# Which engine takes out a weight's sign and in how many bits, what fills the first routing phase, and how the first expert's first products are cut

## The chip, the cores and the metric

The kernel runs on one core of a Trainium2 chip. The metric is the device time of one execution in microseconds (us), median over runs; lower is better. Engines are named as the profile names them: PE (TensorE matmul, PEld its weight load), DVE (VectorE), ACT (ScalarE), POOL (GpSimd), SP (SyncE, which here only starts DMAs).

## The reference, cut to what matters

```python
x = attention(q, k, v)                  # 4 x 8 heads x 576 rows, window of 64; -> 2304 tokens x 512
logits = x @ w_gate                     # 8 experts, at most 288 tokens each
# all (token, expert) pairs in order of falling logit; a token goes to the first expert with room
out[mask_e] = relu(x[mask_e] @ w1[e]) @ w2[e]          # expert: 512 -> 1024 -> 512
h = out @ w_in                          # 512 -> 2048
y = maximum(0.01 * h, h) @ w_out        # 2048 -> 512, the output
```

`w_in` and `w_out` come to the kernel as 64-bit floats. The kernel has to make 32-bit floats of them on the chip.

## The kernel before, in words

**Attention** comes first, in 18 chunks of 128 tokens (to about 96 us). Then one list of steps is walked (`Moe.run`, L982): expert 0 (8 steps), expert 1 (8), block 0 of the last layer (16 steps, 512 tokens), experts 2 and 3, block 1, and so on. A step is `hstep` (first product and its non-linearity, `h` then `hh`) and `ystep` (second product, into `ya` for an expert, `oa` for a block). PE gets `h` of step i+1 before the second product of step i. Expert 0 multiplies in plain f32; all later steps split both factors into a high and a low part (ACT casts the high part, DVE or POOL subtracts it) and add three products.

**Routing** is worked out in 8 phases, one expert per phase (`Router.phase`, L357). A phase is a chain: six times DVE compares (`r_ge`), PE counts in 18 small matmuls (`rp`), DVE compares with the room left (`r_sat`), PE, DVE (`r_ns`); then prefix sums, and at the end the token numbers (`ids`). Expert 0 cannot begin before phase 0 has ended: its rows are gathered (`xg`, POOL DMAs), transposed on PE (`xtp`), copied by ACT (`xT`), and only then multiplied. Phase 1 runs during expert 0, phases 2 and 3 during expert 1 and block 0.

**Conversion** (`Convert`, L587) turns the 64-bit weights into 32-bit ones in 32 units of 128x512, two per step of a block. A unit arrives in a `cv_in` tile (4 of them) as pairs of 32-bit words, low and high. `open` (L617) has three ACT operations: k=0 scales the high word, read as f32, by 2^-112 into the result; k=1 takes the top byte of the low word and writes the three missing bits; k=2 writes the scaled result as f16, whose only surviving bit is the sign. Both k=1 and k=2 write 16 bits each into halves of the same 32-bit word. `join` (L644) is one DVE operation: result shifted left by 3, or that word. Units 0, 1, 4, 5, 8, 9 and 12 to 17 (`KEPT`) are converted in place, then cast by ACT (`cast`) and their low part taken by DVE (`low`) into `res`. The other twenty get one of six `cv_r` tiles, are split in block 0 (`split`, L761) and sent to DRAM (`wsp`); a tile is free again when the unit six before it was split. Units 0 to 2 are done during attention (`spare`, L691), unit 3's ACT operations at its end.

**The order of the work** is planned when the kernel is built. `Clocks` (L1089) keeps a modelled time per engine from a cost per operation; `Convert.acts` opens units and issues casts while ACT's modelled time is no more than 200 ns ahead; `Convert.piece` issues one `join` or `low` on DVE if its inputs are due. `RouteDriver.tick` (L1200), called between groups of matmuls, chooses between split low parts, routing and conversion pieces. `RouteDriver.finish` (L1224) runs routing phases that must be complete, and in phases 0 and 1 calls `nfill` pieces at marked points. Each engine takes its instructions strictly in the order issued, so an instruction that waits holds back all behind it on that engine. No conversion loads are issued from the end of phase 0 (`hold`) until step 2 of expert 0. Nearly all instructions after attention are recorded under one line, L1158, so the rows are read by tile names.

Of the kernel before, what the change touches and what calls it, by code (L numbers as in the profile page):

```python
# [6 lines left out]
F32 = mybir.dt.float32  # L7
F32R = mybir.dt.float32r
BF = mybir.dt.bfloat16
I32 = mybir.dt.int32  # L10
AF = mybir.ActivationFunctionType
ALU = mybir.AluOpType
# [542 lines left out]
    return out  # L555


U8, U16, F16 = mybir.dt.uint8, mybir.dt.uint16, mybir.dt.float16

def lay_w12(w1, w2):  # L560
    a = w1.reshape(NE, 4, 128, 8, 128).transpose(0, 3, 2, 1, 4).reshape(NE, 8, 128, 512)
# [18 lines left out]
NRING = 6  # L580
# [6 lines left out]
class Convert:  # L587
# [5 lines left out]
    def __init__(self, nc, pool, wio, res):  # L593
        self.nc, self.pool, self.wio, self.res = nc, pool, wio, res
        self.st, self.nl, self.done, self.hold = {}, 0, 0, False
        self.side = nc.scalar.copy, nc.vector
        self.out, self.taken, self.due, self.came, self.now = {}, set(), [], {}, lambda: 0
        self.left, self.joined, self.relief = {}, [], lambda: None
    def load(self, eng=None):
        n = self.nl  # L600
        if n >= 32 or self.hold:
# [15 lines left out]
    def open(self, n):  # L617

        if n not in self.out:
            while n not in self.st:  # L620
                self.load()
            self.out[n], self.left[n] = self.room(n), [2, 1, 0]
        t, o, act = self.st[n], self.out[n], self.nc.scalar.activation
        half = t.rearrange("p a b -> p (a b)").bitcast(F16).rearrange("p (a b) -> p a b", b=4)
        k = self.left[n].pop()
        if k == 0:
            act(o, t[:, :, 1].bitcast(F32), AF.Copy, scale=float(2.0 ** -112))
        elif k == 1:
            act(half[:, :, 0].bitcast(U16), t.bitcast(U8)[:, :, 3], AF.Copy, scale=1 / 32, bias=-31 / 64)
        else:  # L630
            act(half[:, :, 1], o, AF.Copy)
    def done_at(self, ap):
# [10 lines left out]
        self.load()  # L643
    def join(self):  # L644
        n = self.done
        o = self.out[n].bitcast(I32)
        self.nc.vector.scalar_tensor_tensor(out=o, in0=o, scalar=3, in1=self.st.pop(n)[:, :, 0], op0=ALU.logical_shift_left, op1=ALU.bitwise_or)
        self.done += 1
        if n in KEPT:
            self.joined.append(n)  # L650
        else:
            self.load()
# [23 lines left out]
    def until(self, n):  # L676
        while self.done < min(n, 32):
            u = self.done
            if u not in self.out and not self.free(u):
                self.relief()  # L680
                self.finish(u)
            while u not in self.out or self.left[u]:
                self.open(u)
            self.join()
        self.finish(n)
    def finish(self, n):
        while self.joined and self.joined[0] < n:
# [3 lines left out]
    def spare(self, n):  # L691

        g, v, act = self.nc.gpsimd, self.nc.vector, self.nc.scalar.activation
        while self.done < n:
            k = self.done
            t, o = self.st[k], self.room(k)
            self.out[k], self.left[k] = o, []
            lo, hi, oi = t[:, :, 0], t[:, :, 1], o.bitcast(I32)
            half = t.rearrange("p a b -> p (a b)").bitcast(F16).rearrange("p (a b) -> p a b", b=4)
            act(o, hi.bitcast(F32), AF.Copy, scale=float(2.0 ** -112))  # L700
            yield
            act(half[:, :, 0].bitcast(U16), t.bitcast(U8)[:, :, 3], AF.Copy, scale=1 / 32, bias=-31 / 64)
            yield
            act(half[:, :, 1], o, AF.Copy)
            yield
            v.scalar_tensor_tensor(out=oi, in0=oi, scalar=3, in1=lo, op0=ALU.logical_shift_left, op1=ALU.bitwise_or)
            del self.st[k]
            yield
            if k in KEPT:
                w = self.res[KEPT.index(k)]  # L710
                g.tensor_copy(w[:, 0], o)
                yield
                g.tensor_tensor(out=w[:, 1], in0=o, in1=w[:, 0].bitcast(F32), op=ALU.subtract)
            self.load()
            yield
            self.done += 1
# [2 lines left out]
XM = 4, 3, 2  # L719
PAIR = 2  # L720
ELOW, MLOW = 1, 1
WARM, CVG = 11, 2
XW = 5200
class Moe:
    def __init__(self, nc, tc, ctx, ident, pp_misc, pa, pp, w12, wsp, xd, idl, out, route):
# [80 lines left out]
    def xtrans(self, n, a):  # L806
        nc = self.nc
        if a == 0:
            self.xT[n] = [self.wk.tile([128, 3, 4, 96], F32R, tag=f"xT{d}", name=f"xT{n}_{d}", bufs=1) for d in range(2)]
        hi, lo = self.xT[n]  # L810
        self.route.flush(("x", n))
        g = self.xg.pop((n, a))
        if n < 2 and n + a == 2 or a == 1 and (n % 2 or n == 0):
            pt = self.pp.tile([128, 4, 96], F32, tag="h", name=f"xtp{n}_{a}")
        else:
            pt = self.misc.tile([128, 4, 96], F32, tag="xt", name=f"xtp{n}_{a}", bufs=1)
        for k in range(4):
            nc.tensor.transpose(pt[:, k, :], g[:, 128 * k:128 * k + 128], self.ident[0:96, 0:96])
        if n == 0:
            nc.scalar.copy(hi[:, a].bitcast(F32), pt)  # L820
            return
        nc.scalar.copy(hi[:, a], pt)
        self.route.later(("x", n), hi, lambda: nc.vector.tensor_tensor(out=lo[:, a], in0=pt, in1=hi[:, a].bitcast(F32), op=ALU.subtract))
    def mslots(self, n):
        return 512 * n, 512 if n < 4 else 256
    def hprod(self, i, hi):

        nc = self.nc
        kind, n, p, f = self.seq[i]
        lo = self.hdone.get(i, 0)  # L830
        self.hdone[i] = hi
        if i not in self.ph:
            self.ph[i] = self.pp.tile([128, 512], F32, tag="h", name=f"h{i}")
        ph, w = self.ph[i], self.w[i, 0]
        self.route.flush(("w", i, 0))
        if kind == "e":
            self.route.flush(("x", n))
        if kind == "e" and n == 0:
            for k in range(4):
                nc.tensor.matmul(ph[:, :288].rearrange("p (a c) -> p a c", a=3), w[:, 128 * k:128 * k + 128], self.xT[n][0][:, :, k].bitcast(F32), start=(k == 0), stop=(k == 3))  # L840
                self.route.tick()
            return
        whi, wlo = w[:, 0], w[:, 1]
        if kind == "e":
            N = 288
            rh, rl = ([x[:, :, k, :] for k in range(4)] for x in self.xT[n])
        else:
            s0, N = self.mslots(n)
            pos = s0 % RING
            rh, rl = ([y[k][pos // 512][:, pos % 512:pos % 512 + N] for k in range(4)] for y in self.Y)  # L850
        o = ph[:, :N].rearrange("p (a c) -> p a c", a=3) if kind == "e" else ph[:, :N]
        prods = [x for k in range(4) for x in ((whi, rh, k), (whi, rl, k), (wlo, rh, k))]
        if (lo, hi) != (0, 12) or p == 0:

            prods.sort(key=lambda x: x[1] is rl)
        for j, (w, r, k) in enumerate(prods):
            if lo <= j < hi:
                nc.tensor.matmul(o, w[:, 128 * k:128 * k + 128], r[k], start=(j == 0), stop=(j == 11))
                if j % 3 == 2:
                    self.route.tick()  # L860
# [121 lines left out]
    def run(self):  # L982
        nc, seq, R = self.nc, self.seq, self.route
# [23 lines left out]
            self.conv.piece()  # L1007
        for a in range(3):
            self.xtrans(0, a)
        self.hstep(0)  # L1010
        self.split(2, 0)
        self.split(1, 1)
        for i in range(n):
# [9 lines left out]
            for m in range(1, 8):  # L1023
# [9 lines left out]
                        self.xtrans(m, a)  # L1033
                if i == first[m] - 1 and seq[i][0] == "e":
                    self.xtrans(m, 2)
            if i == 2:

                self.conv.hold = False
                while len(self.conv.st) < 3:
                    self.conv.load()  # L1040

            for j in range(i + 1, i + 6 if self.ng > 1 else min(i + 6, first[1] + 2)):
# [42 lines left out]


CVA, CV0, CVL = 3, 8, 3
AHEAD, SOON, ASLACK = 2, 150, 200
class Clocks:  # L1089


# [18 lines left out]
    def cost(self, e, name, out, ins):  # L1110
# [5 lines left out]
            return max(n[0] * (1.68 if ins[0].dtype == F32 and ins[1].dtype == F32 and ins[1].shape != ins[0].shape else 0.447) + 1, 25)  # L1116
        n = max(n)
        if e == "scalar":
            return n * 0.833 + (55 if psum else 93)
        if e == "gpsimd":  # L1120
            return n * 2.2 + 98
        big = [x for x in ins if x.shape[-1] > 1]
# [38 lines left out]
class RouteDriver:  # L1161
# [38 lines left out]
    def tick(self):  # L1200
        for _ in range(4):
            t, dve = self.nc.at["tensor"], self.nc.at["vector"]
            one = self.ph == 1
            go = [j for j in self.jobs if j[1] <= max(t, dve)]
            go = [j for j in go if not isinstance(j[0], tuple)] or go
            soon = [j for j in self.jobs if not isinstance(j[0], tuple) and j[1] <= max(t, dve) + self.HOLD]
# [17 lines left out]
    def finish(self, ph, known=None):  # L1224

        k = 0
        while 'ids' not in self.out.get(ph, ()):
            self.piece()
            if known and ph in self.out:
                known()  # L1230
                known = None
            k += 1
            if ph <= 1:
                for _ in range(self.nfill):
                    self.conv.piece()

def build(nc, tc, qT, kT, v, vT, wg, cfd, cid, cbd, w12, wio, out):
    with ExitStack() as ctx:
# [65 lines left out]
        pm = ctx.enter_context(tc.tile_pool(name="pm", bufs=1, space=PSUM, reuse_waits="tile"))  # L1304
        ph = ctx.enter_context(tc.tile_pool(name="m_ph", bufs=2, space=PSUM, reuse_waits="tile"))
        nc = cv.nc = rt.nc = Clocks(nc)
        cv.side = nc.scalar.copy, nc.vector
        cv.now = lambda: max(nc.at["tensor"], nc.at["vector"])
        R = RouteDriver(nc, rt, cv)
# [29 lines left out]
```

## Time and profile before

| | us |
|---|---|
| median of 3 runs | 840.31 (838.67 to 843.12) |
| the profiled execution, time | 840.8 |
| its span, first to last instruction | 839.1 |
| PE busy | 770.2 (92%) |
| DVE busy | 437.6 (52%) |
| ACT busy | 380.5 (45%) |

In the stage tables a row gives the stretch in us from the span's start, its length, the busy time of each engine with the number of instructions, the granted TensorE clock as a share of 2.4 GHz, the DMA share and GB/s. In a timeline a row gives the start, the duration, the engine, the operation with its output and input tiles and count, and in brackets how long the engine sat idle before it and what ended that.

### The profile page before, as it was taken

How to read it: one execution, taken by the hardware profiler on the slowest of the kernel's cores; microseconds unless marked ns; L12 is line 12 of the kernel's file. 1: busy time of each engine (PE TensorE's matmuls, PEld its weight loads, DVE VectorE, ACT ScalarE, POOL GpSimd, SP SyncE). 2: the span in 40 equal slices, each digit the busy share in tenths (PEclk: the TensorE clock that was granted, in tenths of full speed). 3: DMA queues.
4: the chain of work that ended last, by engine and by line, in shares of the span. 5: the costliest groups of instructions: out<-in, count | busy, mean ns of one | idle time of the engine just before them, and what ended most of it. 6: DMA issues, size and time to landing. Idle time of an engine off the chain costs nothing.

```text
span 839.1 us, 15086 instructions
## 1 busy us (share of the span) xinstructions
PE 770.2 (92%) x5828; PEld 639.0 (76%) x5829; DVE 437.6 (52%) x1191; ACT 380.5 (45%) x771; POOL 138.9 (17%) x165
## 2 busy tenths in 40 slices
PE   6987629979988989999999999999999999999996
PEld 4765425668866668899777789998888998888896
DVE  3656685668865677697766833322223323222332
ACT  5788991177686663342211134532124453221222
POOL 2323002010010000300000027720004761000200
PEclk9999855999999999999999999999999999999999
DMA  9994243565464445848322428682243935223652
GB/s 346 411 405 151 75 143 125 176 200 131 126 231 157 142 176 176 163 151 172 121 81 76 151 93 177 191 226 74 104 178 110 216 93 209 101 101 121 234 197 102
DMA packets 44728, 138.70 MB, mean 165 GB/s; under 512 B 9712, under 2 KB 10608, under 8 KB 44656
## 3 DMA queue, kind: packets, MB, share of 16 engines
q1 hardware_dynamic: 40816, 126.36, 45.6%
q0 software_dynamic: 3408, 11.01, 5.1%
q8 instruction: 46, 0.75, 0.4%
q10 hardware_dynamic: 432, 0.36, 0.1%
q14 instruction: 26, 0.21, 0.1%
HBM read 117.78 MB, written 19.93 MB: 164 GB/s over the span
## 4 chain that ended last, share of the span: by engine, by line
PE 48%; DVE 6%; issue 5%; DMA 5%; ACT 4%; POOL 1%; POOLq 0%; SPq 0%; ACTq 0%
PE h L1158 23%; PE oa L1158 16%; PE ya L1158 6%; DMA raw<-in_w_dram 3%; ACT cv_in L1158 3%; PE rp L1158 2%; DVE w L1158 1%; DVE r_ob L1158 1%; DVE h L1158 1%; DMA out_dram<-ot,sidx 1%; POOL w L1158 1%; DVE hh L1158 1%; DVE cv_r L1158 1%; PE xtp L1158 1%; DMA sidx<-idl 1%
## 5 line engine op out<-in xcount | busy, mean ns | idle before, releaser
L1158 PE MATMUL h<-Y,w 128*128 128x512 f32 (+1 forms) x600 | 139.0, 378 | 0.0
L1158 PE MATMUL oa<-w,hh 128*128 128x512 f32 x540 | 134.2, 393 | 0.0
L1158 ACT COPY tg<-h 128x512 f32<-128x512 f32 (+1 forms) x80 | 44.4, 555 | 191.6 <-PE h L1158 191.6
L1158 DVE SCALAR_TENSOR_TENSOR h<-h,tg 128x512 f32<-128x512 f32 (+1 forms) x80 | 51.6, 644 | 140.1 <-ACT tg L1158 140.0
L1158 PEld LDWEIGHTS h<-Y,w 128*128 128x128 f32 x600 | 105.6, 190 | 20.9
L1158 PEld LDWEIGHTS oa<-w,hh 128*128 128x128 f32 x540 | 99.8, 188 | 21.9 <-issue 0.8
L1158 PE MATMUL h<-xT,w 128*128 128x288 f32 x672 | 101.8, 298 | 0.9 <-DVE xT L1158 0.9
L1158 POOL TENSOR_TENSOR w<-raw,w 128x512 fp32r<-128x512 f32 x50 | 63.1, 1290 | 228.7 <-DVE xT L1158 117.9
L1158 PE MATMUL ya<-hh,w 128*128 128x288 f32 x672 | 100.7, 297 | 0.2 <-ACT hh L1158 0.2
L1158 PEld LDWEIGHTS h<-xT,w 128*128 128x128 f32 x672 | 92.6, 188 | 2.0 <-DVE xT L1158 1.2
L1158 PEld LDWEIGHTS ya<-hh,w 128*128 128x128 f32 x672 | 91.7, 188 | 1.9 <-ACT w L1158 1.2
L1158 PE MATMUL oa<-res,hh 128*128 128x512 f32 x324 | 84.0, 403 | 0.0
L1158 PE MATMUL h<-Y,res 128*128 128x512 f32 (+1 forms) x360 | 83.1, 374 | 0.9 <-ACT Y L1158 0.9
L1158 ACT ACTIVATE hh<-h 128x288 fp32r<-128x288 f32 (+1 forms) x64 | 26.3, 411 | 114.8 <-PE h L1158 114.2
L1158 PEld LDWEIGHTS h<-Y,res 128*128 128x128 f32 x360 | 62.4, 188 | 13.8 <-ACT Y L1158 1.1
L1158 ACT CAST hh<-h 128x512 fp32r<-128x512 f32 (+1 forms) x80 | 43.5, 544 | 63.6 <-DVE h L1158 61.9
L1158 DVE TENSOR_TENSOR hh<-h,hh 128x512 fp32r<-128x512 f32 (+1 forms) x80 | 51.0, 637 | 38.2 <-ACT hh L1158 36.2
L1158 PEld LDWEIGHTS oa<-res,hh 128*128 128x128 f32 x324 | 60.2, 191 | 13.3 <-ACT hh L1158 0.3
L1158 ACT CAST w<-raw 128x512 fp32r<-128x512 f32 x112 | 63.8, 618 | 8.1 <-DMA raw<-in_w_dram 8.1
L1158 DVE SCALAR_TENSOR_TENSOR hh<-h,hh 128x288 fp32r<-128x288 f32 x56 | 25.4, 454 | 67.1 <-ACT hh L1158 66.9
L1158 ACT ACTIVATE cv_in<-cv_in 128x512 uint16<-128x512 uint8 (+2 forms) x48 | 56.5, 1221 | 0.3
L1158 POOL DMA_INDIRECT out_dram<-ot,sidx x18 | 18.5, 1030 | 229.1 <-DMA w<-wsp 93.5
(162 smaller groups left out, 950.5 us busy)
## 6 DMA issues: line engine op xcount, KB each, us to landing
w<-wsp SPq DMA_DIRECT2D x80, 512.0 KB, 4.1
raw<-in_w_dram SPq DMA_DIRECT2D x61, 512.0 KB, 4.5
cv_in<-in_wio_dram SPq DMA_DIRECT2D x32, 512.0 KB, 4.5
wsp<-w SPq DMA_DIRECT2D x20, 512.0 KB, 2.9
avo<-in_v_dram SPq DMA_DIRECT2D x6, 876.0 KB, 9.7
aq<-in_q_dram SPq DMA_DIRECT2D x12, 384.0 KB, 8.8
avt<-in_vt_dram SPq DMA_DIRECT2D x6, 768.0 KB, 9.9
xd<-ax SPq DMA_DIRECT2D x18, 256.0 KB, 6.0
```

Of the source, the lines that this page charges most:

```text
L1158: return f(*a, **kw)
```

## The change

Four things change. **Sign and low bits:** k=1 now writes a whole 32-bit word; for units below 18 ACT still writes the sign over its upper half, for units 18 to 31 (and 0 to 2) that ACT operation goes and DVE does a second operation (sign bit of the high word, or the result). Units 0 to 2 get a `cv_r` tile in `spare`. **No filler in phase 0:** `finish` calls only `acts` there; the pieces come after it, up to 8 in place of 2, and in phase 1 where `tick` finds a marked wait. The hold ends at step 0, not step 2. **Thirds:** after each 96 rows are transposed, steps 0 and 1 of expert 0 do their first products for those rows. **Planner:** an f16 result costs ACT 2.9 times more, the fixed cost is 140, ACT starts at 7000 ns, units are opened 3 ahead.

```diff
@@ Convert.open
-            self.out[n], self.left[n] = self.room(n), [2, 1, 0]
+            self.out[n], self.left[n] = self.room(n), [2, 1, 0] if n < BYACT else [1, 0]
@@
-            act(half[:, :, 0].bitcast(U16), t.bitcast(U8)[:, :, 3], AF.Copy, scale=1 / 32, bias=-31 / 64)
+            act(t[:, :, 0], t.bitcast(U8)[:, :, 3], AF.Copy, scale=1 / 32, bias=-31 / 64)
@@ Convert.join
+        o, t, v = self.out[n].bitcast(I32), self.st[n], self.nc.vector
+        if n not in self.half:
+            v.scalar_tensor_tensor(out=o, in0=o, scalar=3, in1=t[:, :, 0], op0=ALU.logical_shift_left, op1=ALU.bitwise_or)
+            self.half.add(n)
+            if n >= BYACT:
+                return
+        else:
+            v.scalar_tensor_tensor(out=o, in0=t[:, :, 1], scalar=-0x80000000, in1=o, op0=ALU.bitwise_and, op1=ALU.bitwise_or)
+        del self.st[n]
@@
-WARM, CVG = 11, 2
+WARM, CVG = 11, 8
@@ Moe
+    def hthird(self, i, a):
+        if i not in self.ph:
+            self.ph[i] = self.pp.tile([128, 512], F32, tag="h", name=f"h{i}")
+        for k in range(4):
+            self.nc.tensor.matmul(self.ph[i][:, 96 * a:96 * a + 96], self.w[i, 0][:, 128 * k:128 * k + 128], self.xT[0][0][:, a, k].bitcast(F32), start=(k == 0), stop=(k == 3), skip_group_check=True)
+        self.hdone[i] = 12
@@ Moe.run
         for a in range(3):
             self.xtrans(0, a)
+            self.hthird(0, a)
+            self.hthird(1, a)
         self.hstep(0)
@@
-            if i == 2:
+            if i == 0:
                 self.conv.hold = False
-                while len(self.conv.st) < 3:
+                while len(self.conv.st) + len(self.conv.joined) + len(self.conv.due) < 4:
                     self.conv.load()
@@
-AHEAD, SOON, ASLACK = 2, 150, 200
+AHEAD, SOON, ASLACK, BYACT = 3, 150, 200, 18
@@ Clocks.cost
-            return n * 0.833 + (55 if psum else 93)
+            return n * 0.833 * (2.9 if out.dtype == F16 else 1) + (55 if psum else 140)
@@ RouteDriver.tick
+            if one and self.mode == 'v' and self.nfill:
+                self.nfill = 0
+                self.conv.piece()
@@ RouteDriver.finish
-            if ph <= 1:
+            self.conv.acts()
+            if ph == 1:
                 for _ in range(self.nfill):
                     self.conv.piece()
@@ build
+        nc.at["scalar"] = 7000.0
```

## Rows read from the trace of the kernel before

**Rows 1.** Busy time by stretch: routing phase 0, expert 0's start, expert 0, expert 1, block 0, rest
```profile
96.60:127.40 30.80, 8.06 (x120) 6.35 (x120) 22.45 (x81) 28.29 (x50) 0.61 (x2) 0.54 0.43 146
127.40:145.30 17.90, 16.17 (x76) 9.65 (x75) 8.72 (x28) 2.35 (x5) 4.87 (x6) 0.56 0.37 122
145.30:179.40 34.10, 33.13 (x229) 23.57 (x228) 20.79 (x77) 12.87 (x18) 2.84 (x3) 1.00 0.53 173
179.40:218.40 39.00, 34.18 (x303) 31.00 (x302) 32.36 (x87) 27.87 (x48) 0.00 (x0) 1.00 0.58 144
218.40:339.60 121.20, 108.67 (x603) 83.95 (x603) 83.10 (x223) 78.66 (x113) 4.31 (x6) 0.96 0.50 172
340.00:800.00 460.00, 458.58 (x2827) 396.60 (x2826) 203.18 (x520) 146.70 (x302) 95.23 (x95) 1.00 0.49 144
```

**Rows 2.** Timeline of phase 0: PE's small matmuls behind r_sat, first and last of six
```profile
97.69 0.16 PE L1158 MATMUL rp<-r_sat,pow 63*128 63x8 bf16 x1 [1.01 <-DVE r_sat L1158]
...
105.58 0.16 PE L1158 MATMUL rp<-r_sat,pow 63*128 63x8 bf16 x1 [4.55 <-DVE r_sat L1158]
...
109.00 0.16 PE L1158 MATMUL rp<-r_sat,pow 31*128 31x8 bf16 x1 [1.53 <-DVE r_sat L1158]
...
116.11 0.16 PE L1158 MATMUL rp<-r_sat,pow 31*128 31x8 bf16 x1 [0.32 <-DVE r_sat L1158]
```

**Rows 3.** Timeline of DVE at the second r_sat and behind phase 0
```profile
104.77 0.69 DVE L1158 SCALAR_TENSOR_TENSOR cv_in<-cv_in 128x512 int32<-128x512 int32 x1 [4.34 <-issue]
...
133.13 1.28 DVE L1158 TENSOR_TENSOR res<-cv_in,res 128x512 fp32r<-128x512 f32 x2
```

**Rows 4.** Timeline of the start of expert 0: PE, then ACT
```profile
132.94 1.54 PE L1158 MATMUL xtp<-cft,xg 96*128 96x96 f32 x8
135.43 0.90 PE L1158 MATMUL xtp<-cft,xg 96*128 96x96 f32 x4 [0.95 <-DMA xg<-xd,r_ids]
...
138.28 5.63 PE L1158 MATMUL h<-xT,raw 128*128 128x288 f32 x12
...
144.51 0.75 PE L1158 MATMUL h<-xT,raw 128*128 128x288 f32 x2
...
127.26 0.65 ACT L1158 CAST res<-cv_in 128x512 fp32r<-128x512 f32 x1 [0.56 <-DVE cv_in L1158]
133.93 1.07 ACT L1158 COPY xT<-xtp 128x384 f32<-128x384 f32 x2 [6.02 <-PE xtp L1158]
```

**Rows 5.** Groups by shape: xcount | busy us, mean ns | idle before, releaser
```profile
L1158 ACT ACTIVATE cv_in<-cv_in 128x512 uint16<-128x512 uint8 x28 | 37.8, 1351 | 0.0
L1158 ACT ACTIVATE cv_in<-cv_in 128x512 f16<-128x512 f32 x10 | 13.5, 1355 | 0.3
L1158 DVE SCALAR_TENSOR_TENSOR cv_r<-cv_r,cv_in 128x512 int32<-128x512 int32 x19 | 13.1, 690 | 19.6 <-ACT cv_in L1158 19.2 <-ACT cv_in L631 0.4
L1158 ACT ACTIVATE cv_in<-cv_in 128x512 f32<-128x512 f32 x10 | 7.2, 720 | 0.0
```

**Rows 6.** Timeline from expert 0 to expert 1: ACT, then PE
```profile
172.43 5.81 ACT L1158 ACTIVATE cv_in<-cv_in 128x512 uint16<-128x512 uint8 x5
...
182.13 0.55 PE L1158 MATMUL xtp<-cft,xg 96*128 96x96 f32 x4 [2.71 <-DVE xT L1158]
```

**Rows 7.** Waits from 178 to 340 us: us in total, times, longest
```profile
DVE cv_r L1158 <- ACT cv_in L1158: 17.7, 12, 2.7
...
ACT cv_r L1158 <- DVE w L1158: 8.5, 6, 2.5
```

**Rows 8.** Timeline of PE in block 0: the longest waits, and matmuls behind two of them
```profile
237.19 0.54 PE L1158 MATMUL rp<-r_ob,r_rhs 128*6 128x96 bf16 x9 [2.82 <-DVE r_ob L1158]
255.93 0.65 PE L1158 MATMUL rp<-r_oh,r_ge 128*63 128x8 bf16 x9 [2.41 <-DVE r_ge L1158]
256.50 3.40 PE L1158 MATMUL oa<-res,hh 128*128 128x512 f32 x8
...
310.13 0.57 PE L1158 MATMUL rp<-r_ob,r_rhs 128*6 128x96 bf16 x9 [2.57 <-DVE r_ob L1158]
```

More of the change, by code (lines that the diff above doesn't have):

```diff
@@ L555, in make_pow2 @@
     return out
-U8, U16, F16 = mybir.dt.uint8, mybir.dt.uint16, mybir.dt.float16
+U8, F16 = mybir.dt.uint8, mybir.dt.float16
 def lay_w12(w1, w2):
@@ L597, in __init__ @@
         self.out, self.taken, self.due, self.came, self.now = {}, set(), [], {}, lambda: 0
-        self.left, self.joined, self.relief = {}, [], lambda: None
+        self.left, self.joined, self.half, self.relief = {}, [], set(), lambda: None
     def load(self, eng=None):
@@ L645, in join @@
         n = self.done
-        o = self.out[n].bitcast(I32)
-        self.nc.vector.scalar_tensor_tensor(out=o, in0=o, scalar=3, in1=self.st.pop(n)[:, :, 0], op0=ALU.logical_shift_left, op1=ALU.bitwise_or)
+        o, t, v = self.out[n].bitcast(I32), self.st[n], self.nc.vector
[7 more added lines that the diff above has]
+        del self.st[n]
         self.done += 1
@@ L683, in until @@
                 self.open(u)
-            self.join()
+            while self.done == u:
+                self.join()
         self.finish(n)
@@ L695, in spare @@
             k = self.done
-            t, o = self.st[k], self.room(k)
+            t, o = self.st[k], self.pool.tile([128, 512], F32, tag="cv_r", name=f"cv_r{k}", bufs=NRING)
             self.out[k], self.left[k] = o, []
             lo, hi, oi = t[:, :, 0], t[:, :, 1], o.bitcast(I32)
-            half = t.rearrange("p a b -> p (a b)").bitcast(F16).rearrange("p (a b) -> p a b", b=4)
             act(o, hi.bitcast(F32), AF.Copy, scale=float(2.0 ** -112))
             yield
-            act(half[:, :, 0].bitcast(U16), t.bitcast(U8)[:, :, 3], AF.Copy, scale=1 / 32, bias=-31 / 64)
-            yield
-            act(half[:, :, 1], o, AF.Copy)
+            act(lo, t.bitcast(U8)[:, :, 3], AF.Copy, scale=1 / 32, bias=-31 / 64)
             yield
             v.scalar_tensor_tensor(out=oi, in0=oi, scalar=3, in1=lo, op0=ALU.logical_shift_left, op1=ALU.bitwise_or)
+            yield
+            v.scalar_tensor_tensor(out=oi, in0=hi, scalar=-0x80000000, in1=oi, op0=ALU.bitwise_and, op1=ALU.bitwise_or)
             del self.st[k]
@@ L812, in xtrans @@
         g = self.xg.pop((n, a))
-        if n < 2 and n + a == 2 or a == 1 and (n % 2 or n == 0):
+        if n == 0:
+            pt = self.pa.tile([128, 4, 128], F32, tag="acc", name=f"xtp{n}_{a}", bufs=4)[:, :, :96]
+        elif n < 2 and n + a == 2 or a == 1 and n % 2:
             pt = self.pp.tile([128, 4, 96], F32, tag="h", name=f"xtp{n}_{a}")
@@ L838, in hprod @@
         if kind == "e" and n == 0:
+            if lo:
+                return
             for k in range(4):
```

## The prediction

> **What bounds the kernel now.** I read the busy time by stretch first, then the timelines and waits inside the stretches where PE is not full. From 340 to 800 us PE is busy 458.6 of 460 us at full clock [rows 1]: what is saved ahead of that moves the end by as much, and nothing behind it can give much. The room lies in four stretches. In phase 0 of the routing PE works 8 of 30.8 us, since nothing else can run until the first expert's tokens are known. Expert 0's start (17.9 us) is PE-bound but at a granted clock of 0.56, so mostly at 1.2 of 2.4 GHz. Expert 0 itself is full: 33.1 of 34.1 us. Expert 1 leaves PE idle 39.0 - 34.2 = 4.8 us, and block 0 leaves 121.2 - 108.7 = 12.5 us, with a clock of 0.96 [rows 1].
>
> Who holds PE there? In phase 0, DVE: PE waits for `r_sat` six times [rows 2], and in the worst case DVE sat 4.34 us idle before a conversion's join that stood ahead of `r_sat` [rows 3]. In block 0 the list of waits says that DVE waited 17.7 us in 12 pieces for ACT's conversion of a unit [rows 7]; behind such joins stand `r_ob`, `r_ge` and `hh`, and PE's longest stalls (2.82, 2.41, 2.57 us) end on these [rows 8]. DVE is not full in block 0 (83.1 of 121.2 us), ACT is not either (78.7) [rows 1]: it is the order that hurts. The planner books 512 x 0.833 + 93 = 520 ns for each of ACT's conversion operations, where those that write 16 bits last 1351 and 1355 ns [rows 5]. So it places joins on DVE long before ACT is done, and DVE, strictly in order, stands.
>
> **Part by part.**
>
> *No filler in phase 0.* The least wait for `r_sat` is 0.32 us, the last of six; I take that as the wait without interference. The first three give back (1.01 - 0.32) + (4.55 - 0.32) + (1.53 - 0.32) = 6.1 us [rows 2]; the others are short. Nothing covers this chain and nothing else in it moves: **-6.1 us** (ends -5 and -6.6). ACT still opens units 4 and 5 in phase 0, which no routing step waits for. The price is moved work: before, eight joins and four low parts were over by about 135 us; now only three joins and two low parts fit (loads are held, so units 3, 4 and 5 are all there is). Seven operations of 0.69 us [rows 5], 4.8 us, go later. I cost them at nothing: DVE is idle 34.1 - 20.8 = 13 us in expert 0 [rows 1], the new pieces of phase 1 are put at points where DVE waits for PE, and the units for them are loaded from step 0 on, not step 2. If that cover is gone they come in block 0, at 4.8 us (a rival, below). The earlier loads stand on SP's queue ahead of the weights of steps 5 and later; those can't start anyhow before a `raw` tile is free, so I charge nothing.
>
> *Thirds, and what stands ahead of them.* Before, the products of steps 0 and 1 begin when all three thirds are there, and end at 144.51 + 0.75 = 145.3, with some 0.9 us of routing matmuls among them [rows 4]. Now the joins of units 3 to 5 follow `r_sat` on DVE at 133.1 (0.64 us each, the pitch of the two low parts there [rows 3]), the casts of 4 and 5 queue on ACT behind those, 0.65 us each, and ahead of the first copy of `xT`, which thus starts near 135.7 and not 133.9 [rows 4]. Then each third costs 16 matmuls of 96 columns. The transposes have 96 columns too: 1.54 / 8 = 0.19 us each at this clock [rows 4], so 3.1 us a third; three of these are 9.1 us, against 16 x 5.63 / 12 = 7.5 us for the whole products [rows 4]. Between thirds come four transposes (0.9) and a copy that PE now waits for (0.48 and some 0.25 of hand-over). In the old time scale: first third 136.2 to 139.3, second 140.9 to 144.0, third from 145.6; with the full clock by then half of 3.1, to 147.2. Against 144.4 that is **+3.0 us**, rounded up for hand-overs. Ends: 0, if the casts don't delay the copies and thirds fill the wait for the last gather (0.95 us [rows 4]); +6, if the new waits put off the rise of the clock, as the last third and the next products then stay at half speed. I take the middle, since the casts are in order ahead of the copies by the code.
>
> *Low bits as whole words.* No row shows a byte read and a 32-bit write by ACT. The upper end is the row itself, 1351 ns: nothing gained. The lower is ACT's 32-bit read and write at the same stride of 8 bytes, 720 ns [rows 5]. I take 0.72: f16 written from 32-bit input lasts as long as 16 bits written from bytes (1355 against 1351), so what is slow is what those two share, the 16-bit write. The Trainium skill, "ScalarE: Activation LUTs", section "What ACT_TABLE_LOAD costs", has one element per cycle for every function in fp32 and bf16 alike, with 186 ns on top for immediates. By that all three operations would last about 613 ns as they are and this part would give nothing; the trace has 1351, so measurement decides, but the page leaves open what the slow half is.
>
> *Sign.* Fourteen units lose an ACT operation of 1.36 us (19.0 us) and gain a DVE one of 0.69 us (9.7 us) [rows 5], nearly all in block 0, and their low bits get 14 x 0.63 = 8.8 us shorter. ACT in block 0 thus falls by some 28 of its 78.7 us; DVE goes to 83.1 + 9.7 = 92.8 us [rows 1].
>
> *Planner.* With 2.9 times for f16 it books 1376 ns, with the rest 566 ns, close to the rows. So joins go where ACT is done. I give: expert 1, whose 2.71 us stall follows 5.81 us of ACT conversions ahead of `hh` and `xT` [rows 6], gets back 3.2 of its 4.8 us: **-3.2** (ends -1 and -4.8). Block 0 gets back the three long stalls, 7.8 us [rows 8]; and the clock with them: a mean of 0.96 over 121.2 us is 121.2 x 0.08 = 9.7 us at half speed, 4.8 us lost, and the slow matmuls stand behind those stalls (eight took 3.40 us right after one [rows 8]). Of the 9.7 us of DVE signs I charge 2.6 back, a quarter and a bit, as DVE is then at 92.8 / 111 = 84% and `hh` queues more often: **-10.0** (ends -17.3, all of idle and clock, and +9.7, all signs in PE's way). What is late next is DVE itself; routing phase 3 has no user until expert 3, so it can slip.
>
> Sum: -6.1 + 3.0 - 3.2 - 10.0 = -16.3 us. The profiled execution took 840.8, which gives 824.5; the median is 0.5 lower, so **824.0 us**.
>
> **Rivals.** *The byte read is the slow part:* the low-bits operation stays at 1.35 us, and the planner, which now books 0.57 for it, still places joins too early, by 0.8 us a unit instead of 1.7. Then expert 1 and block 0 give half: -6.1 + 3.0 - 1.6 - 5.0 = -9.7, 830.6 us. For it: no row separates read from write. Against it: the f16 rows. 17%. It too is what is left if the page's rule on element rate held for reads alone.
>
> *Units late:* the seven operations moved out of phase 0 don't find room in expert 0, block 0 begins with fewer units joined, and the forced conversions there stand in PE's way. Also ACT waits 8.5 us for DVE's split of the unit six before [rows 7], a ring that faster ACT operations don't speed up. Block 0 gives nothing and 4.8 comes on top: -6.1 + 3.0 - 3.2 + 4.8 = -1.5, 838.8 us. Against: DVE's idle 13 us in expert 0. 14%.
>
> *DVE takes ACT's place:* in block 0 each second join stands in the line `tg`, `h`, `hh` that PE's second product waits for. This decides from where DVE has no idle time between a step's `h` and `hh`; at 84% it may. With all 14 on the path and no gain in expert 1 or block 0: -6.1 + 3.0 + 9.7 = +6.6, 846.9 us, slower. Against: from 340 on PE is full with DVE work beside it, and the planner knows DVE's cost. 11%.
>
> **How the numbers follow.** The forecast has 58%. A measurement of this kernel tells about 0.5%, 4.2 us, from no change: the forecast and the first rival are faster (75%), late units count as the same (14%), DVE as the bound as slower (11%). The forecast's own range, with -5 to -15 for block 0 and 0 to +6 at the start, is 816 to 832. The range of 8 in 10 goes from 814 to 840, which takes in the first two rivals and leaves the third out.
>
> **What would show it.** Right: `ids` of phase 0 some 6 us earlier and no `cv` joins between its `r_sat` rows; ACT rows int32<-uint8 near 0.7 us; the wait of DVE for ACT's `cv_in` from 17.7 us to under 5; PE idle in block 0 at 4 to 6 us and no clock below 0.98 there; expert 0's step 1 product ending 3 us later counted from `ids`. Wrong: int32<-uint8 at 1.3 us (first rival); joins of units 18 and on still running in the last steps of block 0 with PE behind them (second); PE's waits in block 0 ending on DVE `hh` or `h` with DVE over 95% busy (third); or the first products as early as the phase was shortened, in which case my term for the thirds is wrong.

## The result, and the profile after

The changed kernel takes **816.18 us** (median of 4 runs, 813.27 to 816.45) against 841.71 us (4 runs, 838.67 to 843.19) of the kernel before on the same chip: a ratio of 0.9693, interval 0.9655 to 0.9732, or 25.5 us less. The forecast was 824.0 us, 16.3 us less. Direction and range hold; several terms have the wrong size, and one is missing.

To see where the time went I cut both profiled executions at the same events: PE's first matmul behind `r_sat`, `ids` of phase 0, the first second product (`ya`) of expert 0, the first `h` of expert 1, the first `h` of block 0, block 0's last `oa`. First the kernel before, by windows cut there (columns as in [rows 1]):

```profile
97.69:127.22 29.53, 7.81 (x119) 6.26 (x119) 21.51 (x78) 27.05 (x43) 0.61 (x2) 0.52 0.45 152
127.22:145.26 18.04, 16.31 (x76) 9.62 (x75) 8.90 (x30) 2.50 (x5) 4.87 (x6) 0.56 0.37 121
145.26:184.66 39.40, 35.72 (x243) 25.43 (x242) 23.93 (x84) 17.27 (x28) 2.84 (x3) 1.00 0.51 163
184.66:219.27 34.61, 31.64 (x290) 29.18 (x291) 29.56 (x82) 24.34 (x40) 0.00 (x0) 1.00 0.61 151
219.27:339.78 120.51, 108.83 (x604) 84.11 (x605) 82.94 (x222) 77.79 (x111) 4.40 (x6) 0.96 0.50 172
339.78:839.10 499.32, 491.48 (x3033) 426.02 (x3031) 213.86 (x544) 155.88 (x325) 97.33 (x98) 1.00 0.48 143
```

The same windows of the changed kernel:

```profile
89.33:112.24 22.91, 7.78 (x119) 6.24 (x119) 17.06 (x70) 8.71 (x26) 0.61 (x2) 0.51 0.21 78
112.24:134.30 22.06, 18.04 (x89) 14.15 (x89) 7.71 (x22) 3.01 (x6) 4.87 (x6) 0.58 0.44 150
134.30:177.22 42.92, 39.39 (x243) 27.15 (x243) 26.67 (x94) 19.85 (x33) 2.84 (x3) 0.92 0.50 162
177.22:207.25 30.03, 30.03 (x270) 28.52 (x269) 26.05 (x61) 24.24 (x43) 0.00 (x0) 1.00 0.53 153
207.25:309.33 102.08, 102.06 (x588) 79.56 (x587) 86.52 (x212) 58.03 (x106) 3.96 (x5) 1.00 0.65 217
309.33:814.20 504.87, 495.83 (x3091) 428.00 (x3089) 228.94 (x600) 156.32 (x325) 90.94 (x95) 1.00 0.48 142
```

| stretch | before | after | change | forecast |
|---|---|---|---|---|
| attention, to the first `r_sat` | 97.7 | 89.3 | -8.4 | not in the sum |
| phase 0 | 29.5 | 22.9 | -6.6 | -6.1 |
| start of expert 0 | 18.0 | 22.1 | +4.0 | +3.0 |
| rest of expert 0 | 39.4 | 42.9 | +3.5 | 0 |
| expert 1 | 34.6 | 30.0 | -4.6 | -3.2 |
| block 0 | 120.5 | 102.1 | -18.4 | -10.0 |
| the rest | 499.3 | 504.9 | +5.6 | 0 |
| span | 839.1 | 814.2 | -24.9 | -16.3 |

The forecast for expert 1 was made for a stretch that begins 5.3 us earlier ([rows 1], from 179.40); the 2.71 us stall that it names, at 182.13 [rows 6], falls in this table into the rest of expert 0.

What to read in it: in expert 1 and block 0 PE is now busy to the last tenth at full clock, so these cannot give more without less PE work. ACT's time in block 0 fell from 77.8 to 58.0 us while DVE's rose only to 86.5 of 102. Expert 0 got longer in both parts, with a clock of 0.92 in a stretch that had 1.00. And "the rest" got longer because PE does more there.

The conversion's groups by shape of the changed kernel, which answer to [rows 5]:

```profile
L1178 ACT ACTIVATE cv_in<-cv_in 128x512 int32<-128x512 uint8 x28 | 18.8, 670 | 0.0
L1178 ACT ACTIVATE cv_in<-cv_in 128x512 f16<-128x512 f32 x10 | 13.7, 1370 | 0.2
L1178 DVE SCALAR_TENSOR_TENSOR cv_r<-cv_r,cv_in 128x512 int32<-128x512 int32 x19 | 13.0, 687 | 1.3 <-ACT cv_in L1178 1.2
L1178 DVE SCALAR_TENSOR_TENSOR cv_r<-cv_in,cv_r 128x512 int32<-128x512 int32 x14 | 9.6, 686 | 0.1
```

Bytes read and whole words written take 670 ns where 16-bit writes took 1351; the f16 write stays at 1370. DVE's idle time ahead of its joins is 1.3 us, from 19.6. The list of waits of block 0 (207 to 310 us) answers to [rows 7], which has 17.7 and 8.5 us for the same two:

```profile
ACT cv_r L1178 <- DVE w L1178: 3.6, 4, 1.6
...
DVE cv_r L1178 <- ACT cv_in L1178: 1.2, 3, 0.6
```

and PE's timeline in phase 0 answers to [rows 2], where the same wait had 4.55 at the worst:

```profile
92.92 0.16 PE L1178 MATMUL rp<-r_sat,pow 63*128 63x8 bf16 x1 [0.25 <-DVE r_sat L1178]
...
101.48 0.16 PE L1178 MATMUL rp<-r_sat,pow 31*128 31x8 bf16 x1 [0.24 <-DVE r_sat L1178]
```

### The profile page after: what moved, and what is told of

The parts are those of the page before. It is cut to its first block, busy times and chain, and to the rows that moved or that the text cites. A ratio compares the mean times of both kernels' runs of the same rounds, so it can differ in the third digit from the quotient of the medians.

```text
span 814.2 us, 15149 instructions
## 1 busy us (share of the span) xinstructions
PE 771.4 (95%) x5860; PEld 642.5 (79%) x5861; DVE 451.0 (55%) x1213; ACT 340.0 (42%) x754; POOL 131.9 (16%) x160
## 4 chain that ended last, share of the span: by engine, by line
PE 77%; DVE 9%; issue 5%; DMA 4%; ACT 3%; POOL 0%; POOLq 0%; SPq 0%; DVEq 0%; ACTq 0%
PE h L1178 34%; PE oa L1178 20%; PE ya L1178 13%; PE rp L1178 5%; DMA avo<-in_v_dram 2%; DVE r_ob L1178 1%; PE ao L161 1%; PE apt L146 1%; ACT ap L141 1%; PE as L128 1%; PE xtp L1178 1%; DVE r_ob_S L1178 1%; DMA sidx<-idl 1%; DVE w L1178 1%; DMA aq<-in_q_dram 1%
## 5 line engine op out<-in xcount | busy, mean ns | idle before, releaser
L1178 PEld LDWEIGHTS h<-Y,w 128*128 128x128 f32 x600 | 103.9, 188 | 20.2
L1178 POOL TENSOR_TENSOR w<-raw,w 128x512 fp32r<-128x512 f32 x45 | 56.7, 1289 | 108.4 <-ACT w L1178 108.4
L1178 POOL DMA_INDIRECT xg<-xd,r_ids x24 | 24.2, 1007 | 194.9 <-DVE r_ac L1178 184.6
```

The lines of the kernel that those rows point to most:

```text
L1178: return f(*a, **kw)
```

## The experiments

The runs were made on three chips, where the kernel before took 847.01 us (runs 1 to 4), 846.41 (5 to 8) and 843.47 (9 to 11); so times are compared by their ratio to it, and stretches by their lengths in the profile. "LAND" is the time after which the planner takes a conversion load to have landed (6000 ns, in both kernels).

| run | ratio to before, interval | attention | phase 0 | start | rest of exp. 0 | exp. 1 | block 0 | rest | span |
|---|---|---|---|---|---|---|---|---|---|
| 1 no thirds | 0.9672 (0.9639 to 0.9704) | 89.4 | 22.9 | 17.3 | 36.7 | 33.9 | 111.0 | 507.1 | 818.3 |
| 2 filler back | 0.9712 (0.9677 to 0.9747) | 90.3 | 23.9 | 18.3 | 43.0 | 31.7 | 108.1 | 504.6 | 819.8 |
| 3 first signs on ACT | 0.9721 (0.9684 to 0.9758) | 99.0 | 22.9 | 22.3 | 41.1 | 30.2 | 102.2 | 505.5 | 823.2 |
| 4 the same, join later | 0.9664 (0.9626 to 0.9702) | 92.8 | 22.9 | 22.1 | 43.0 | 30.0 | 102.1 | 505.2 | 818.0 |
| 5 before, true costs | 0.9951 (0.9933 to 0.9969) | 97.5 | 23.6 | 16.7 | 36.0 | 33.8 | 126.4 | 507.4 | 841.3 |
| 6 all signs on ACT | 0.9713 (0.9697 to 0.9730) | 89.4 | 22.9 | 20.2 | 41.4 | 30.0 | 107.1 | 505.6 | 816.7 |
| 7 routing in thirds | 0.9722 (0.9702 to 0.9741) | 89.2 | 22.9 | 23.5 | 40.5 | 31.6 | 105.7 | 504.8 | 818.3 |
| 8 whole, filler, LAND | 0.9675 (0.9659 to 0.9691) | 89.5 | 23.9 | 18.4 | 43.0 | 32.0 | 104.5 | 505.3 | 816.5 |
| 9 whole, LAND | 0.9630 (0.9615 to 0.9644) | 90.4 | 22.9 | 16.3 | 36.7 | 33.0 | 104.3 | 504.9 | 808.5 |
| 10 thirds, LAND | 0.9638 (0.9622 to 0.9654) | 89.5 | 22.9 | 22.2 | 42.6 | 30.0 | 102.6 | 504.4 | 814.1 |
| 11 changed, again | 0.9659 (0.9636 to 0.9681) | 89.9 | 22.9 | 21.9 | 42.6 | 30.0 | 102.1 | 504.9 | 814.2 |

The ratios of most runs cannot be told from that of the changed kernel (0.9693, and 0.9659 in run 11), as their intervals overlap; what the runs show is read from the stretches, each from one profile.

### Attention: runs 3 and 4

The missing term, -8.4 us, lies where units 0 to 2 are converted between attention's own work. Groups of the kernel before, up to 100 us:

```profile
L706 DVE SCALAR_TENSOR_TENSOR cv_in<-cv_in 128x512 int32<-128x512 int32 x2 | 1.4, 696 | 8.3 <-ACT cv_in L704 8.3
L706 DVE SCALAR_TENSOR_TENSOR cv_r<-cv_r,cv_in 128x512 int32<-128x512 int32 x1 | 0.7, 692 | 3.7 <-ACT cv_in L704 3.7
```

DVE stands 12.0 us in three joins until ACT has written the sign. The changed kernel has no such operation there, and its joins (L711, L713) show 0.0 idle. Two things fell together, ACT's time and DVE's wait; runs 3 and 4 put the sign of these units back on ACT, run 4 with the join one place later:

```diff
@@ Convert.spare
+            act(half[:, :, 1], o, AF.Copy)
+            yield
+            yield                              # run 4 only
             v.scalar_tensor_tensor(out=oi, in0=oi, scalar=3, in1=lo, op0=ALU.logical_shift_left, op1=ALU.bitwise_or)
-            yield
-            v.scalar_tensor_tensor(out=oi, in0=hi, scalar=-0x80000000, in1=oi, op0=ALU.bitwise_and, op1=ALU.bitwise_or)
```

> The changed kernel, but units 0 to 2, which are converted during attention, have their sign written by ACT again (f16) and one join, with the join placed right after that operation as in the kernel before. Attention ended 7.6 us earlier in the changed kernel, which I had not forecast. Theory (the join waits for ACT on DVE, and ACT has 1.4 us more a unit): attention gets 5 to 8 us longer, 821 to 824 us. Rival (the whole-word low bits, 0.65 us a unit, or where the result lies, did it): at most 2 us longer, 816 to 818 us.

> As the run with the sign of units 0 to 2 on ACT, with the join one filler place later. It parts the two halves of that theory: if ACT's own time is what lengthens attention (3 x 1.4 us), it stays 4 us or more above the changed kernel, 820 us and more; if it was DVE standing in a join that waits for ACT, it is within 1.5 us of the changed kernel, 815 to 818 us.

Groups of run 3, up to 100 us, and then of run 4:

```profile
L714 DVE SCALAR_TENSOR_TENSOR cv_r<-cv_r,cv_in 128x512 int32<-128x512 int32 x3 | 2.1, 693 | 10.1 <-ACT cv_in L712 10.1
```

```profile
L715 DVE SCALAR_TENSOR_TENSOR cv_r<-cv_r,cv_in 128x512 int32<-128x512 int32 x3 | 2.1, 684 | 0.0
```

Attention is 9.7 us longer in run 3 and only 3.5 in run 4 (99.0 and 92.8 against 89.3). In the runs that leave this part as changed it is 89.2 to 90.4. So 6.2 us was DVE standing in the join with attention's work queued behind it; the other 3.5 came with the three operations of ACT (4.2 us). The first expectation had the direction and too small a size (5 to 8 us); the second had neither, as 3.5 lies between the two cases it named (4 and more, or under 1.5). By its ratio run 4 is no slower than the changed kernel. The Trainium skill, "Perfetto Trace Analysis", section "Tensor Engine Instruction (MATMUL, LD_WEIGHTS)", calls ACT, DVE and GpSimd strictly first in, first out; the idle time of L714 and its absence in run 4 agree with it.

### Phase 0, and what the planner's costs do alone: runs 2 and 5

```diff
@@ RouteDriver.finish                          # run 2, of the changed kernel
-            if ph == 1:
+            if ph <= 1:
@@ Clocks                                      # run 5, of the kernel before
-    return n * 0.833 + (55 if psum else 93)
+    return n * 0.833 * (2.9 if out.dtype in (F16, U16) else 1) + (55 if psum else 140)
+        nc.at["scalar"] = 7000.0
```

> The changed kernel with the conversion pieces back in routing phase 0. Theory (my term): every join or low part ahead of r_sat costs what it cost before, phase 0 gets 6 us longer, 821 to 823 us. Rival (they hurt only because joins were placed before ACT was done; the planner now knows ACT's cost and start): the phase gets at most 2 us longer, and expert 0 and block 0 have that work behind them, 814 to 818 us.

> The kernel before, with nothing changed but the planner's numbers: 2.9 times for both 16-bit operations of ACT, 140 ns fixed, ACT starting at 7000 ns. Theory (order): the stalls came from joins placed on DVE before ACT was done, so the same instructions in an honest order give back most of phase 0 (29.5 to about 24 us) and at least half of block 0's 18 us; ratio to before 0.975 to 0.985. Rival (ACT's own time is the bound in block 0, three 16-bit operations for every two units): phase 0 gets shorter but block 0 stays above 115 us; ratio 0.99 to 1.0. Attention stays at 97.7 us in both, since its order isn't planned.

With filler back, phase 0 takes 23.9 us, 1.0 longer: for this stretch the rival held. For the whole it did not: the span is 819.8 us, 5.6 above the changed kernel's, with block 0 at 108.1, 6.0 longer, and the start 3.8 shorter. With true costs alone and filler in, the kernel before does phase 0 in 23.6 where it took 29.5. So filler was nearly harmless to the phase where it was placed after ACT had done its part; what cost some 6 us was filler booked too early. Part of this is that the true costs place less of it there: joins and low parts between the first and the last `r_sat` are five in the kernel before, three in run 2, two in run 5. My number for this term came true for the wrong reason.

In block 0 run 5 did the opposite of what the theory of order asked: 126.4 us, longer than the 120.5 before, and the ratio is the rival's. Its window, and PE's longest waits there:

```profile
207.54:333.94 126.40, 107.99 (x566) 82.84 (x567) 81.19 (x202) 93.21 (x127) 4.00 (x5) 0.93 0.56 184
```

```profile
PE oa L1158 <- ACT hh L1158: 8.7, 3, 7.8
PE oa L1158 <- DVE hh L1158: 5.4, 1, 5.4
```

ACT has 93 us of work in it, and `hh` stands behind it. Knowing the true cost does not remove it: conversions that are put off come due all the same. Without cheaper operations the planner's part is worth 0.5% in all (ratio 0.9951).

### Sign on DVE: run 6

```diff
-BYACT = 3, 150, 200, 18
+BYACT = 3, 150, 200, 32
```

> The changed kernel with the sign of units 18 to 31 on ACT again (f16 operation, one join); all else as changed. Theory (order is what counted; ACT has room once the low bits are whole words): within 2 us of the changed kernel, ratio to before 0.968 to 0.972. Rival (ACT's 19 us matter): block 0 gets 4 to 8 us longer, ratio 0.974 to 0.980. My forecast charged 2.6 us for the sign on DVE; if that is real, this run is up to 2.6 us faster.

The ratio, 0.9713, lies in the range of the theory of order, the block in that of the rival: 107.1 us, 5.0 longer, with 3.4 us given back in expert 0 (61.6 against 65.0). The block's own row, PE's one wait in it, and DVE's wait for ACT's conversions in this block and then in that of run 5, answering to [rows 7]:

```profile
203.95:311.07 107.12, 103.96 (x588) 80.45 (x587) 82.10 (x216) 75.14 (x120) 4.22 (x5) 0.98 0.63 210
...
296.11 3.81 PE L1178 MATMUL oa<-w,hh 128*128 128x512 f32 x10 [3.16 <-ACT hh L1178]
...
DVE cv_r L1178 <- ACT cv_in L1178: 10.9, 9, 2.6
...
DVE cv_r L1158 <- ACT cv_in L1158: 34.7, 14, 5.2
```

ACT has 17 us more than in the changed kernel, DVE 4 us less, PE is idle 3.2 us, all of it in one wait for ACT's `hh` with ten slow matmuls behind. So the last 5.0 us of block 0's gain are the signs that left ACT; DVE's second operation costs nothing that shows, since in the changed block 0 no wait of PE is listed at all.

The other 13.4 us (120.5 to 107.1) run 6 already has, with 75.1 us of ACT work in the block, hardly less than the 77.8 before. So the amount of ACT's work does not explain these; DVE's waits for it did fall, from 17.7 to 10.9 us. Against run 5, which has the same true costs, ACT has 18.1 us less in the block, 13.6 of it in the low bits (24.3 to 10.7 us), and the block is 19.3 shorter. That fits low bits as what made the true costs pay, but run 6 also has the moved filler, the thirds and units opened 3 ahead. No run has the low bits with the old planner, or with the true costs alone: which of these edits gave the 13.4 us is not shown.

### Thirds: runs 1, 7, 8, 9, 10 and 11

Runs 1, 8 and 9 take the two calls of `hthird` out. Run 8 also puts the filler back, runs 8 to 10 book loads later; run 7 lets routing in between the thirds; run 11 is the changed kernel again.

```diff
@@ Moe.run
-            self.hthird(0, a)                  # runs 1, 8, 9
-            self.hthird(1, a)
+            R.tick()                           # run 7, behind the two calls
@@
-LAND = 6000
+LAND = 9000                                    # runs 8, 9, 10
```

> The changed kernel without the products by thirds: steps 0 and 1 of expert 0 are multiplied whole, after all three transposes. Theory (thirds cost): in the changed kernel the product of step 1 ends 22.3 us after the token numbers of phase 0, against 18.1 us before, and phase 1's first count waits 14.5 us on PE behind the thirds, so that expert 1's rows arrive 2.7 us late and eight matmuls run at half clock. Without thirds: 6 to 8 us faster than the changed kernel, 808 to 810 us, and no PE wait for xg. Rival (thirds fill the wait for the gathers, what came later has other causes): 816 to 819 us.

Run 1 shortened expert 0 by 11.0 us (54.0 against 65.0) and gave 8.9 of it back in block 0 and 3.9 in expert 1. No wait for `xg` was left, as its theory said, but the time was not 6 to 8 us less: its span is 818.3 us against 814.2. Where it lost time in block 0, in the timeline of ACT, PE and SP's queue:

```profile
207.49 0.66 ACT L1176 ACTIVATE cv_r<-cv_in 128x512 f32<-128x512 f32 x1 [5.09 <-DMA cv_in<-in_wio_dram]
...
210.56 5.35 PE L1176 MATMUL oa<-res,hh 128*128 128x512 f32 x12 [4.54 <-ACT hh L1176]
...
203.44 0.33 SPq L799 DMA_DIRECT2D wsp<-w  x1
204.04 0.74 SPq L605 DMA_DIRECT2D cv_in<-in_wio_dram  x1
```

A load of a unit started only at 204.04, behind a store on SP's queue; ACT, to which the planner had given it as landed, waited 5.09 us for it; `tg` and `hh` were queued behind, PE stood 4.54 us and then ran twelve matmuls in 5.35 us (0.45 each; on the changed kernel's page the same group takes 0.397).

> The changed kernel without thirds, with the filler pieces in phase 0, and with 9 instead of 6 us booked for a conversion load. Without thirds, one PE stall of 4.5 us in block 0 stood behind ACT waiting for a load that SP had issued late, behind a store of wsp. Theory: start as short as without thirds (17 us or less, as the casts are done in phase 0), expert 0 36 to 37, block 0 back to 102 to 104; ratio 0.953 to 0.960. Rival (the stalls in block 0 are another wait, the ring of cv_r): block 0 stays at 108 to 111 us, ratio 0.965 to 0.970.

> The changed kernel with the first products in one piece again, no filler in phase 0, and loads of units booked at 9000 ns, not 6000. Theory (what the thirds cost and what a load that comes late costs are two separate things, 6 to 8 us ahead of block 0 and 4 to 9 us in it): start of expert 0 17 to 18 us, its rest 36 to 37.5, block 0 102 to 105 with no wait of PE behind a load; span 805 to 811, ratio to the kernel before 0.953 to 0.961. Rival (whatever is put back or moved, the lists of work are re-made, and the time lost goes elsewhere: with later loads the gathered rows come late again in expert 0, as in the run with filler and later loads): expert 0's rest 41 us or more, or block 0 108 or more; ratio 0.965 to 0.972.

> The changed kernel with one call of the routing between the thirds, so that phase 1's first matmul stands behind the first third on PE and not behind all three. Theory (the thirds cost in expert 0 because phase 1 starts 14 us late there): expert 0's steps from its first second product take 37 to 39 us instead of 42.9, no wait for xg; 3 to 6 us of the span, unless block 0's order loses some of it. Rival (the clock and the extra weight loads cost it): 42 us and more.

> The changed kernel as it is, but for loads of units booked at 9000 ns. Theory (the load that comes late is a matter of the kernel without thirds, where the steps fall otherwise; with thirds no PE wait in block 0 ends on a load): nothing to gain, each stage within 1 us of the changed kernel's, ratio to it within 0.3%. Rival (booking the loads later changes the lists everywhere): expert 0 or block 0 moves by 3 us or more, either way.

> The changed kernel itself, unaltered, beside the other runs of this call on the same chip: ratio to the kernel before 0.966 to 0.973 as the first comparison gave, stages as in its first profile within 1 us each. It says how far one profile of this kernel may be read: a stage that moves by more than 1 us here makes the readings of that stage worth as much less.

Booking loads at 9000 ns takes block 0 to 104.5 and 104.3 us in runs 8 and 9: that wait is gone. It changes no stretch by more than 0.6 us where the thirds are in (run 10), as its theory said. Run 11 repeats the stretches of the changed kernel within 0.6 us. Run 8 missed its ratio, as the rest of expert 0 stayed at 43.0; run 9, the same but for the filler, has 36.7 there. Run 9 has the lowest time: 811.39 us (810.26 to 814.43, 5 runs) against 815.57 (810.62 to 817.33, 6 runs) of run 11 on the same chip, with intervals of the ratios that just overlap. Its ratio missed the expected 0.953 to 0.961, its span of 808.5 met 805 to 811. The thirds alone are the difference of runs 10 and 9: 11.8 us in expert 0 (64.8 against 53.0) and 5.6 net by the profiles (814.1 - 808.5), but those are the slowest of five runs of the one and the fastest of five of the other. By the medians it is 2.5 us (813.91 against 811.39), and the intervals overlap almost whole. So that thirds lengthen expert 0 where phase 0 has no filler is shown, in two pairs of runs (1 and 11, 9 and 10); that they cost time in all is not.

Why thirds lengthen expert 0: the start in the changed kernel, PE, ACT and DVE.

```profile
120.90 3.73 PE L1178 MATMUL h<-xT,raw 128*128 128x96 f32 x16 [2.66 <-ACT xT L1178]
...
125.83 3.73 PE L1178 MATMUL h<-xT,raw 128*128 128x96 f32 x16 [0.57 <-ACT xT L1178]
...
130.77 3.73 PE L1178 MATMUL h<-xT,raw 128*128 128x96 f32 x16 [0.57 <-ACT xT L1178]
...
135.45 0.18 PE L1178 MATMUL rp<-r_sat,pow 63*128 63x8 bf16 x1
...
119.20 1.26 ACT L1178 CAST res<-cv_in 128x512 fp32r<-128x512 f32 x2 [21.10 <-DVE cv_in L1178]
120.36 0.48 ACT L1178 COPY xT<-xtp 128x384 f32<-128x384 f32 x1
...
135.67 0.17 DVE L1178 TENSOR_REDUCE r_ns<-rp 128x1 int32<-128x8 f32 x1 [14.48 <-PE rp L1178]
```

The three thirds are 11.2 us of PE, where 16 whole products take 7.5 at nearly this clock ([rows 4], a granted 0.56): every weight is loaded three times. The windows of 5 us, first of the changed kernel, then of run 9, show that and the clock:

```profile
125.00:130.00 5.00, 4.43 (x22) 4.08 (x20) 0.00 (x0) 0.48 (x1) 0.00 (x0) 0.50 0.04 15
130.00:135.00 5.00, 4.43 (x20) 3.92 (x18) 0.00 (x0) 1.30 (x3) 0.00 (x0) 0.50 0.00 0
135.00:140.00 5.00, 5.00 (x25) 3.27 (x24) 2.37 (x8) 0.00 (x0) 0.00 (x0) 0.74 0.15 32
```

```profile
125.00:130.00 5.00, 5.00 (x33) 3.44 (x33) 1.69 (x6) 0.82 (x2) 0.00 (x0) 0.86 0.60 244
130.00:135.00 5.00, 5.00 (x37) 3.37 (x35) 2.54 (x10) 0.18 (x1) 0.00 (x0) 1.00 0.32 105
135.00:140.00 5.00, 5.00 (x52) 3.31 (x51) 2.27 (x8) 3.69 (x6) 0.00 (x0) 1.00 0.25 63
```

With thirds, PE has a weight load beside it for 3.92 of 5 us (0.22 us each), stops 0.57 us for each copy of `xT`, and runs at 1.2 GHz until past 135; in run 9 it has 2.4 GHz from 130 on, and the start takes 16.3 us. The second cost is behind it. PE takes its matmuls in order, so the first `pow` of routing phase 1 comes behind all thirds at 135.45, and DVE's `r_ns` waits 14.48 us for it; in run 9 the same matmul runs at 123.45. The phase ends late (its `ids` come 31.4 us after the first `ya`, in run 9 24.3), and expert 1's rows with it, on PE's timeline of the changed kernel:

```profile
170.49 1.16 PE L1178 MATMUL xtp<-cft,xg 96*128 96x96 f32 x8 [2.72 <-DMA xg<-xd,r_ids]
171.48 3.82 PE L1178 MATMUL ya<-hh,raw 128*128 128x288 f32 x8
175.47 2.13 PE L1178 MATMUL ya<-hh,raw 128*128 128x288 f32 x8
```

PE waits 2.72 us for the gathered rows, and the eight matmuls behind that wait take 3.82 us, not 2.13: the clock of 0.92 in the table. Run 7 let routing in between the thirds and got only 2.4 us of this back (40.5), at 1.4 more for the start: its theory, 37 to 39 with no wait for `xg`, fell short, as PE still waited 1.23 us for `xg`. Its rival, 42 and more, did not hold either.

In run 8 the chain of phase 1 begins at 125.30 and `ids` come at 157.00, in run 9 at 123.45 and 153.83; with filler the gathered rows then come 2.76 us late, without it in time. Up to the first `ya` filler takes 3.1 us (42.3 against 39.2), and the rest of expert 0 is then 6.3 longer. The late chain is the smaller part of that: counted from the first `ya`, `ids` come 25.3 us later in run 8 and 24.3 in run 9. Why the gathers themselves also take longer in run 8 stays open; the window from its first gather to the first rows (157.43 to 164.77) has a DMA share of 0.93, that of run 9 up to its transposes (154.26 to 160.52) 0.76.

With filler in phase 0 the thirds cost nothing in expert 0: run 2 has them and run 8 does not (and books loads later), and the start is 18.3 against 18.4, the rest 43.0 in both. In run 2 one cast, not two, stands ahead of the first copy, and the clock rises before the last third. That third and its window in run 2, and then the same window of run 6:

```profile
130.61 2.02 PE L1178 MATMUL h<-xT,raw 128*128 128x96 f32 x16 [0.57 <-ACT xT L1178]
...
130.00:135.00 5.00, 4.43 (x28) 3.62 (x28) 1.53 (x7) 1.30 (x3) 0.00 (x0) 1.00 0.00 0
...
130.00:135.00 5.00, 4.43 (x27) 3.61 (x27) 1.52 (x6) 1.30 (x3) 0.00 (x0) 1.00 0.00 0
```

The last third takes 2.02 us there, and in run 6 too, whose start is 20.2. So what the thirds cost hangs on what stands around them, the clock included.

## Why the prediction was right or wrong

**Attention (missing, -8.4 us).** The sum begins at phase 0. The step that failed is the count of units under *Sign* ("Fourteen units lose an ACT operation"): I counted units 18 to 31 and left out 0 to 2, which the change also moves. The 12.0 us of idle time of L706 was there to be read.

**Phase 0 (-6.6, forecast -6.1).** Right in size. Wrong in reason: "the wait without interference" was taken as work without filler; runs 2 and 5 have filler and phases of 23.9 and 23.6 us, so nearly all the interference came from filler planned on a false cost.

**Thirds (+4.0, forecast +3.0).** Inside the ends of 0 and +6. Mis-sized: 96-column products at 0.19 us, from the transposes, where they took 3.73 / 16 = 0.23; and the clock, which I let rise by the third third and which rose only behind it, my reason for the upper end. In run 6 it did rise by then, behind the same waits (2.66, 0.57 and 0.57 us), so that assumption could have come true. The casts ahead of the copies, for which I moved the whole start, cost nothing by themselves: in run 9 the same two casts stand ahead of the copies, and the start takes 16.3 us. There the wait for the last gather covers them; with thirds it does not, hence the 2.66 (0.78 in run 2, with one cast).

**Rest of expert 0 (+3.5, forecast 0).** I charged the thirds for PE's time alone and did not ask what is queued behind them on PE: phase 1's chain. Without thirds this stretch is 36.7 us in runs 1 and 9, 2.7 less than before, which is the size of the stall of 2.71 us [rows 6]; so thirds took 6.2 here.

**Low bits (0.72, measured 0.670).** Right, and the first rival is out. The Trainium skill, "ScalarE: Activation LUTs", section "What ACT_TABLE_LOAD costs", has one element per cycle and 186 ns for immediates, an estimate of 613 ns by that page; the operation that writes words is now near it, while the f16 one at 1370 is not.

**Expert 1 (-4.6, forecast -3.2).** Near in size, but not by the stall that I named: that one lies in the rest of expert 0, and there the 2.72 us wait for `xg` has taken its place. Of the 4.6 us, 3.0 are PE's idle time behind the first `h` (34.61 - 31.64, now 0), and 1.6 are PE's own work that is no longer in the stretch, 0.9 of it routing matmuls (4.34 to 3.41 us).

**Block 0 (-18.4, forecast -10.0).** Of the 18.4 us, 11.7 are PE's idle time (120.51 - 108.83, now 0.02), 2.5 are routing matmuls that left the block (10.65 to 8.19 us), and 4.2 are left for the clock (0.96 to 1.00). I had given 7.8 to idle time and 4.8 to the clock. Two steps failed. The 2.6 us charged for DVE's signs were not paid: DVE is at 85%, and PE has no wait. And "it is the order that hurts" is half the truth: true costs alone made the block longer (run 5, 126.4 us), and all edits but the sign made it 107.1 (run 6). Which of those edits made the planner's costs pay stays open; the last 5.0 us are ACT's time for the signs. The third rival, DVE in ACT's place, is thereby out; so is the second, as no conversion makes PE wait.

**The rest (+5.6, forecast 0).** That phase 3 "can slip" was right, but it is not free. Routing's matmuls behind block 0 went from 19.36 to 22.79 us, and where PE is full they take their own time; PE's busy time rose by 4.4 in all.

The errors sum to -8.4 - 0.5 + 1.0 + 3.5 - 1.4 - 8.4 + 5.6 = -8.6 us, the difference between 24.9 and 16.3. That the time stayed in the range of 816 to 832 us is luck: attention and block 0 gave 16.8 us more than forecast, both parts of expert 0 and the stretch behind block 0 took 10.1 of it back, and 816.18 lies 0.2 us inside the lower end. As a fall from 840.3 the range ends at 24.3 us, less than the 25.5 measured.

## What to carry to other kernels

Cost every place in which an edited helper runs, the stretches that are full included, and look there for idle time of an in-order engine ahead of the edited operation. Before pricing a piece of work that is put into a chain, list what is queued behind it on its engine, and whether products that are cut smaller load their weights more often. When work is moved out of a stretch, charge it in the one that takes it if the bound engine is full there.

## What the runs showed of the hardware that was not expected

A product cut to 96 columns cost 0.233 us at 1.2 GHz, little over its weight load (3.92 / 18 = 0.22 us in the window from 130 to 135); by columns it would have been a third of 5.63 / 12 = 0.469 us [rows 4], 0.156. At 2.4 GHz, in run 2, it cost 2.02 / 16 = 0.126 us.

The same thirds, behind the same waits of 2.66, 0.57 and 0.57 us, were granted 0.50 from 130 to 135 in the changed kernel and 1.00 in run 6; run 9, with whole products and no wait from 125 on, was granted 0.86 from 125 to 130 and then 1.00. No run shows what made the clock of the changed kernel rise later.
